# Splitting 32 TensorE products ahead of the branch: four tiles of the first batch from 512 to 256 columns, one pair of output tiles from 256 to 128

## The chip, the core and the metric

The kernel runs on one core of a Trainium2 chip. Its five engines run programs of their own and meet at semaphores: PE is TensorE (with PEld, its weight loads), DVE is VectorE, ACT is ScalarE, POOL is GpSimd, SP is SyncE, which here only issues transfers. The metric is the device time of one execution in microseconds (us), lower being better; the figure for a kernel is the median of its runs.

## The reference

The inputs are q, k and v (4 batches, 8 heads, 768 positions, 64 columns), a sorting network `sort_net` (4, 8, 8, 8), and the weights of a gated block. All is float32; the kernel multiplies in bfloat16.

```python
P = sort_net                                   # five Sinkhorn rounds
for _ in range(5):
    P = np.exp(P - P.max(-1)); P = P / P.sum(-1); P = P / P.sum(-2)
k_sorted = einsum('bhij,bhjcd->bhicd', P, k_b) # mixes the 8 blocks of 96 positions
v_sorted = einsum('bhij,bhjcd->bhicd', P, v_b)
attn = softmax(q_b @ k_sorted.T / 8) @ v_sorted   # inside each block of 96
x = attn as (4, 768, 512)
h = relu(x @ w_in)                             # 512 -> 1024 columns: u | v
v_n = layer norm of v over its 512 columns
gated = u * (w_spatial @ v_n + b_spatial)      # mixes the 768 positions
out = gated @ w_out                            # (4, 768, 512)
```

## The kernel before

The whole program is written out, with no loop on the chip. A string `ORDER` lists units, one word each (`VP:15:D:0:4`), and a Python function `u_XX` emits the instructions of each; the order in the string is the order in which every engine's own instructions stand. Four batches overlap: while one is in its attention, the one before it is in the gated block.

The units that matter here:

- **VP and VH** (`u_VP`, matmuls at L566) compute the v half of `x @ w_in` for one tile of 128 positions, 512 columns, as four products over the contraction that add up in one bank of PSUM. With `parts=2`, which is what VH asks for, the 512 columns are done as two runs of 256, each with its own four products and weight loads. Then one relu takes the 512 columns to SBUF, on ACT (L128) or on DVE (L130). Four of the six tiles of batch 0 are VP; the other 20 tiles of the kernel are VH.
- **OP** (`u_OP`, matmuls at L650) computes two tiles of 128 positions of `gated @ w_out`. Its last argument is the number of runs into which the 512 columns are cut: 2 everywhere.
- **SC** (L453) are scores, **AT** (L499) the products with the sorted v, **UP** (L612) the u half, **SP** and **SH** (L624, L680) the spatial product, **WT** (L535) a transpose of weights, **OH** (L700) the last output tiles of batch 3.

```python
for x in range(2):                     # u_OP
    for c in range(0, DM, w):          # w = 512 / parts
        for mc in range(FC):           # FC = 4
            nc.tensor.matmul(t[:, x, c:c + w], lhsT=gt[mc] of tile n0 + x, rhs=w_out_sb[:, mc, c:c + w],
                             start=(mc == 0), stop=(mc == FC - 1))
```

Every product has a weight load of its own in front of it, so a product that is cut in two becomes four instructions in place of two.

**The branch.** The kernel skips the maximum in the softmax, and the five-round network is checked afterwards: `CF` and `LF` (L746 to L751) turn the extreme values into a flag that every engine reads into a register. At `IF` in the string each engine compares and branches (L814). The usual path is the list behind `IF` (units OH, OI, OJ; on TensorE 36 products at L700 with their 36 weight loads). The other path computes everything again with the safe formulas, and it stands in between: on TensorE it is 1,832 products. The branch to the usual path is therefore a jump over that text. `BH`, at the head of the program (L843 in the profile), gives PE, DVE and ACT a hint that the branch is likely taken.

Of the kernel before, what the change touches and what calls it, by code (L numbers as in the profile page):

```python
# [22 lines left out]
SC:0:0:0:0 L:v:1:0:8 PD:1:0:4 VB:15:D:0:3 SC:3:0:1:0 AT:1:0:2:0 SC:0:0:2:1 AT:2:0:3:0 SC:3:0:0:1 PD:1:4:8 AT:1:0:0:0  # L23
KT:0:A:1:0 XT:14:D:0:0:2 AT:3:0:0:1 SC:1:0:3:1 KT:0:A:1:3 AT:2:0:2:1 VM:1:A:1:0 AT:3:0:3:1 VM:0:A:1:1 VM:2:D:1:3
L:q:1:0:8 VM:1:A:1:2 XT:16:A:0:1:2 L:wv AT:0:0:1:0 XT:17:A:0:1:0 KT:2:D:1:1 KT:1:A:1:2 QT:16:D:1:1 QT:10:D:1:3
QT:11:A:1:2 QT:17:D:1:0 XT:14:D:0:0:0 SC:1:1:1:0 L:wsa SC:0:1:2:1 SC:3:1:2:0 VP:15:D:0:4 ST:0:4 VP:14:D:0:3 L:wu
SC:1:1:0:0 SC:0:1:1:1 VP:15:D:0:1 L:wsb ST:0:3 WT:16:A:1 WT:17:D:0 VP:14:A:0:0 ST:0:1 VH:15:A:0:2 ST:0:0 WT:16:A:2
VC:1:0:4 L:q:2:0:8 VH:17:A:0:5 VC:1:4:8 PD:2:0:4 ST:0:2 ST:0:5 AT:1:1:0:0 LN:0:0:6 AT:0:1:1:0 UP:2:A:0:0:0
UP:3:A:0:1:0 BI LA:0:3 LA:0:4 AT:1:1:2:0 SC:2:1:0:1 UP:0:A:0:1:1 LA:0:1 AT:3:1:2:1 L:v:2:0:8 WT:14:A:3 L:k:2:0:8
LA:0:5 LA:0:2 WW:1:D:4 LA:0:0 SC:0:1:3:1 SC:3:1:3:0 UP:2:A:0:0:1 PD:2:4:8 AT:0:1:3:1 QP:A:2:0 SP:1:0:3 QP:A:2:3  # L30
# [12 lines left out]
OP:1:1:4:2 LA:2:5 SC:3:3:2:0 LA:2:0 LA:2:3 LA:2:1 SC:0:3:3:0 OP:2:1:2:2 AT:3:3:3:0 SP:0:2:1 GT:D:2:1 OE:A:1:4 XD:3:1  # L43
AT:1:3:2:0 SP:3:2:0 SP:0:2:2 CK XD:3:0 GT:P:2:0 OE:A:1:2 SP:2:2:3 VH:1:D:3:5:3 GT:D:2:3 VH:10:D:3:4 UP:3:A:3:1:1 CF:11
VH:12:A:3:2 VH:13:A:3:1 OS:1:2:0:2 LF VH:16:A:3:0 GT:D:2:2 OS:1:0:0:2:A UP:2:A:3:1:0 ST:3:1 ST:3:3 UP:0:A:3:0:0 ST:3:4
ST:3:5 OP:1:2:0:2 ST:3:2 ST:3:0 OP:3:2:4:2 LN:3:0:6 LA:3:3 OE:D:2:0 LA:3:4 OP:2:2:2:2 LA:3:0 LA:3:1 OE:A:2:2 LA:3:5
UP:0:A:3:0:1 OE:A:2:4 LA:3:2 OS:0:2:0:2 SH:12:3:2:0 SH:13:3:3:0 GH:P:3:3:0 SH:16:3:0:0 GH:D:3:2:0 SH:17:3:1:0
GH:P:3:0:0 SH:16:3:1:1 SH:12:3:2:1 OS:2:4 GH:P:3:1:0 SH:13:3:3:1 OS:2:0 GH:D:3:1:1 SH:17:3:0:1 OS:1:4 GH:D:3:3:1
OS:2:2 GH:P:3:0:1 GH:P:3:2:1 IF OH:16:3:2:0:512:0:4 OI:A:3:2:0:512 OH:12:3:3:0:512:0:4 OH:13:3:0:0:512:0:4
# [798 lines left out]
```

## Time and profile before

| what | value |
| --- | --- |
| median of 3 runs | 150.45 us (150.36 to 150.85) |
| the profiled execution, its own time | 150.09 us |
| its span, from the first to the last instruction of the program | 148.3 us |
| mean granted TensorE clock over the span | 0.997 |
| PE busy | 141.5 us, 95% of the span |
| DVE busy | 114.6 us, 77% |
| ACT busy | 85.9 us, 58% |
| POOL busy | 39.1 us, 26% |
| transfers of instructions, queue q8 | 14 of 16 KB each |

The span is 1.8 us shorter than the execution's own time; what lies around it are instructions that are not the kernel's. Busy times of PE are those of pipelined products, each of which is shown longer than the distance to the next one, so the distance between the starts of two products, from the chain of waits, is what a product costs when PE is the limit. The list of transfers has a queue per engine for instructions as well: q8 brings text of 16 KB a piece.

### The profile page before, as it was taken

The numbers are of one execution on the slowest core, as the hardware profiler recorded it, in microseconds if no ns is written. First come the engines' busy times: TensorE is split into PE (matmuls) and PEld (weight loads), VectorE is DVE, ScalarE is ACT, GpSimd is POOL, SyncE is SP. The second block draws the span as 40 slices with busy tenths as digits, with TensorE's granted clock in tenths as the row PEclk, the third lists the DMA queues.
The fourth block names the chain that finished last, engine by engine and source line by source line (L and its number), as shares of the span: only waits on it lengthen the run. The fifth ranks groups of instructions, "written<-read, shape, count | busy, mean of one in ns | idle before, by whom it ended". The sixth has DMA issues, their size and how long they took to land.

```text
span 148.3 us, 4108 instructions
## 1 busy us (share of the span) xinstructions
PE 141.5 (95%) x1691; PEld 100.8 (68%) x1691; DVE 114.6 (77%) x262; ACT 85.9 (58%) x126; POOL 39.1 (26%) x44
## 2 busy tenths in 40 slices
PE   6996999999999999999999999999999999999990
PEld 2445877867776657776877678768866876855760
DVE  3876899979987878867869879999568979846741
ACT  5348998987789547658793428756630055170130
POOL 6700699500000006991002640000003000004620
PEclk9999999999999999999999999999999999999998
DMA  3999999999999999799998999508203507007765
GB/s 93 263 205 203 205 209 201 208 221 242 231 248 216 204 216 241 111 197 223 207 201 162 214 243 254 125 0 85 26 0 76 176 6 277 0 2 301 273 235 197
DMA packets 36933, 25.93 MB, mean 175 GB/s; under 512 B 16624, under 2 KB 34032, under 8 KB 36912
## 3 DMA queue, kind: packets, MB, share of 16 engines
q0 software_dynamic: 14432, 12.19, 51.2%
q1 hardware_dynamic: 20832, 10.96, 31.1%
q10 hardware_dynamic: 1648, 2.49, 4.7%
q8 instruction: 14, 0.23, 0.6%
q14 instruction: 7, 0.06, 0.1%
HBM read 24.78 MB, written 6.29 MB: 210 GB/s over the span
## 4 chain that ended last, share of the span: by engine, by line
PE 83%; DVE 10%; ACT 2%; issue 1%; ACTq 0%; DVEq 0%
PE ps L624 16%; PE ps L566 15%; PE ps L612 14%; PE ps L650 11%; PE ps L680 5%; PE ps L499 4%; PE ps L394 4%; PE ps L453 4%; PE ps L700 3%; PE ps L421 3%; DVE x_sb L507 2%; DVE vb L124 1%; PE ps L529 1%; PE ps L535 1%; PE ps L325 1%
## 5 line engine op out<-in xcount | busy, mean ns | idle before, releaser
L641 POOL TENSOR_TENSOR gt<-z,u_sb 128x768 bf16<-128x768 f32 x7 | 11.4, 1645 | 68.5 <-DVE z L630 55.3
L458 ACT ACTIVATE ex_all<-ps 96x768 bf16<-96x768 f32 x32 | 23.7, 808 | 5.1 <-PE ps L453 4.0
L624 PE MATMUL ps<-wspT,v_sb 128*128 128x384 bf16 x144 | 25.1, 326 | 0.0
L566 PE MATMUL ps<-w_in_sb,xT 128*128 128x256 bf16 (+1 forms) x176 | 23.8, 283 | 0.0
L128 ACT ACTIVATE u_sb<-ps 128x768 bf16<-128x768 f32 x16 | 13.0, 811 | 17.3 <-PE ps L612 17.2
L612 PE MATMUL ps<-xT,w_in_sb 128*128 128x384 bf16 x128 | 23.0, 326 | 0.0
L507 DVE TENSOR_TENSOR x_sb<-ps,rec_all 96x512 bf16<-96x512 f32 x32 | 22.0, 686 | 1.1
L624 PEld LDWEIGHTS <-v_sb 128*128 128x128 bf16 x144 | 13.5, 98 | 8.3
L566 PEld LDWEIGHTS <-xT 128*128 128x128 bf16 x176 | 16.3, 98 | 4.0
L650 PE MATMUL ps<-w_out_sb,gt 128*128 128x256 bf16 x144 | 16.9, 273 | 0.0
L612 PEld LDWEIGHTS <-w_in_sb 128*128 128x128 bf16 x128 | 12.0, 98 | 7.0
L586 DVE BATCH_NORM_STATS2 stats<-v_sb 128x6 f32<-128x512 bf16 x24 | 16.2, 675 | 0.6 <-ACT v_sb L128 0.5
L122 ACT COPY o_sb<-ps 128x1024 f32<-128x1024 f32 (+2 forms) x11 | 8.9, 831 | 13.0 <-DVE z L686 7.0
L630 DVE TENSOR_TENSOR z<-ps,b_bc 128x768 f32<-128x768 f32 x12 | 11.5, 954 | 5.9 <-PE ps L624 5.9
L650 PEld LDWEIGHTS <-gt 128*128 128x128 bf16 x144 | 13.8, 98 | 2.0
L499 PEld LDWEIGHTS <-ex_all 96*128 96x128 bf16 x256 | 11.1, 97 | 2.6
L499 PE MATMUL ps<-vb,ex_all 96*128 96x65 bf16 x256 | 12.4, 193 | 0.1
L122 ACT CAST vm<-ps 128x768 bf16<-128x768 f32 x9 | 6.9, 807 | 9.5 <-PE ps L421 6.9
L693 POOL TENSOR_TENSOR gt<-z,u_sb 128x512 bf16<-128x512 f32 (+1 forms) x5 | 5.2, 1046 | 21.5 <-DVE z L686 21.5
L506 DVE RECIPROCAL rec_all<-ps 96x8 f32<-96x8 f32 x32 | 6.3, 195 | 5.6 <-PE ps L499 5.3
L130 DVE TENSOR_SCALAR v_sb<-ps 128x512 bf16<-128x512 f32 (+1 forms) x12 | 8.7, 727 | 1.6 <-PE ps L566 1.5
L236 PE MATMUL ps<-warm 128*128 128x512 bf16 (+2 forms) x34 | 8.6, 411 | 1.3 <-DVE warm L210 1.3
(100 smaller groups left out, 200.5 us busy)
## 6 DMA issues: line engine op xcount, KB each, us to landing
out_dram<-o_sb SPq DMA_DIRECT2D x7, 512.0 KB, 4.6
v_in<-in_v_dram POOLq DMA_DIRECT2D x4, 768.0 KB, 15.4
k_in<-in_k_dram POOLq DMA_DIRECT2D x4, 768.0 KB, 14.4
vb<-vm SPq DMA_DIRECT2D x24, 99.0 KB, 4.5
q_in<-in_q_dram POOLq DMA_DIRECT2D x3, 768.0 KB, 9.7
ws_in<-in_moe_w_spatial_dram POOLq DMA_DIRECT2D x2, 576.0 KB, 16.3
w_in_sb<-in_moe_w_in_dram POOLq DMA_DIRECT2D x2, 512.0 KB, 13.9
out_dram<-o_sb ACTq DMA_DIRECT2D x2, 512.0 KB, 4.1
```

What stands on the lines that cost most here:

```text
L122: nc.scalar.copy(out=out, in_=in_)
L128: nc.scalar.activation(out=out, in_=in_, func=AF.Relu)
L458: nc.scalar.activation(out=e_tile(b, hp, ih).rearrange("p h (x g) -> p h x g", g=G), in_=t[0:BLK, :, 0:HW].rearrange("p h (g x) -> p h x g ...
L499: nc.tensor.matmul(t[:, hh, ii * VW:ii * VW + D + 1], lhsT=e[:, c:c + 128], rhs=vb[b % 2][:, ih * NI + ii, 2 * hp + hh, 0:D + 1], start=Tr ...
L507: nc.vector.tensor_mul(out=x_sb[:, hp].rearrange("p i (h d) -> p h i d", h=2), in0=tv[:, :, :, 0:D], in1=_raw_ap(rec, 0, [rec.ap[0], [NI, ...
L566: nc.tensor.matmul(t[:, x, c:c + DH // parts], lhsT=st["xT", b][:, n // 3, kc, (n % 3) * 128:(n % 3 + 1) * 128], rhs=w_in_sb[:, kc, DH + c ...
L586: nc.vector.bn_stats(out=stats, in_=st["v_sb", b, n])
L612: nc.tensor.matmul(t[:, x, 0:HW], lhsT=w_in_sb[:, kc, mc * 128:(mc + 1) * 128], rhs=st["xT", b][:, ih, kc, :], start=(kc == 0), stop=(kc = ...
L624: nc.tensor.matmul(t[:, x, 0:HW], lhsT=st["v_sb", b, n][:, mc * 128:(mc + 1) * 128], rhs=wspT[:, 3 * x:3 * x + 3, n, :], start=(n == 0), s ...
L630: nc.vector.tensor_add(out=z.rearrange("p (x c) -> p x c", x=2), in0=t[:, :, 0:HW], in1=b_bc.rearrange("p (x c) -> p x c", x=2),)
L641: eng.tensor_mul(out=gt, in0=st["z", b, mc], in1=u)
L650: nc.tensor.matmul(t[:, x, c:c + w], lhsT=st["gt", b, mc][:, (n0 + x) * 128:(n0 + x + 1) * 128], rhs=w_out_sb[:, mc, c:c + w], start=(mc = ...
```

## The change

Five words of the string are changed; no function is.

```diff
-QT:11:A:1:2 QT:17:D:1:0 XT:14:D:0:0:0 SC:1:1:1:0 L:wsa SC:0:1:2:1 SC:3:1:2:0 VP:15:D:0:4 ST:0:4 VP:14:D:0:3 L:wu
-SC:1:1:0:0 SC:0:1:1:1 VP:15:D:0:1 L:wsb ST:0:3 WT:16:A:1 WT:17:D:0 VP:14:A:0:0 ST:0:1 VH:15:A:0:2 ST:0:0 WT:16:A:2
+QT:11:A:1:2 QT:17:D:1:0 XT:14:D:0:0:0 SC:1:1:1:0 L:wsa SC:0:1:2:1 SC:3:1:2:0 VH:15:D:0:4 ST:0:4 VH:14:D:0:3 L:wu
+SC:1:1:0:0 SC:0:1:1:1 VH:15:D:0:1 L:wsb ST:0:3 WT:16:A:1 WT:17:D:0 VH:14:A:0:0 ST:0:1 VH:15:A:0:2 ST:0:0 WT:16:A:2
...
-ST:3:5 OP:1:2:0:2 ST:3:2 ST:3:0 OP:3:2:4:2 LN:3:0:6 LA:3:3 OE:D:2:0 LA:3:4 OP:2:2:2:2 LA:3:0 LA:3:1 OE:A:2:2 LA:3:5
+ST:3:5 OP:1:2:0:2 ST:3:2 ST:3:0 OP:3:2:4:2 LN:3:0:6 LA:3:3 OE:D:2:0 LA:3:4 OP:2:2:2:4 LA:3:0 LA:3:1 OE:A:2:2 LA:3:5
```

The four tiles 4, 3, 1 and 0 of batch 0 take 8 products of 256 columns in place of 4 of 512. The tiles 2 and 3 of batch 2's output take 32 products of 128 columns in place of 16 of 256. The columns that stream through the array stay the same in number; 32 weight loads and 32 products are added, all of them ahead of `IF`. The rows of DVE, ACT, POOL and SP are the same before and after; those of PE go from 7052 to 7116.

PE in the first batch, at tile 4, behind the scores (xT holds the turned attention output, w_in_sb the weights, ps the bank that it adds up in):

```order
 L453 MATMUL ps_73<-qT_679,kt_all_100 128x6x16
 L566 LDWEIGHTS xT_536
-L566 MATMUL ps_73<-w_in_sb_92,xT_536 128x512
+L566 MATMUL ps_73<-w_in_sb_92,xT_536 128x256
...
+L566 LDWEIGHTS xT_536
+L566 MATMUL ps_73<-w_in_sb_92,xT_536 128x256
 L453 LDWEIGHTS kt_all_100
```

The products of a tile are halved in width, and as many again, each with its load, stand behind them before the next scores.

PE in the output of batch 2, tiles 2 and 3 (gt are the four gated chunks, w_out_sb the weights), before:

```order
L650 LDWEIGHTS gt_2085
L650 MATMUL ps_73<-w_out_sb_94,gt_2085 128x256
L650 LDWEIGHTS gt_2029
L650 MATMUL ps_73<-w_out_sb_94,gt_2029 128x256
L650 LDWEIGHTS gt_2191
L650 MATMUL ps_73<-w_out_sb_94,gt_2191 128x256
```

and now:

```order
L650 LDWEIGHTS gt_2101
L650 MATMUL ps_73<-w_out_sb_94,gt_2101 128x128
L650 LDWEIGHTS gt_2045
L650 MATMUL ps_73<-w_out_sb_94,gt_2045 128x128
L650 LDWEIGHTS gt_2207
L650 MATMUL ps_73<-w_out_sb_94,gt_2207 128x128
```

The four chunks are walked through four times for each tile in place of twice, at half the width.

PE at the branch and at the head of the usual path (v_sb is the normed v, wspT the turned spatial weights, spread and u_sb belong to the other path), before; now they are the same but for buffer numbers:

```order
L680 LDWEIGHTS v_sb_2119
L680 MATMUL ps_73<-wspT_93,v_sb_2119 128x256
L814 COMPARE_AND_BRANCH
L266 LDWEIGHTS spread_77
...
L814 UNCONDITIONAL_BRANCH
L700 LDWEIGHTS gt_2341
L700 MATMUL ps_73<-w_out_sb_94,gt_2341 128x512
```

The compare stands in row 3313 of PE before and in row 3377 now; the first row of the usual path moves from 6979 to 7043. Both move down by 64 rows and keep their distance.

## Prediction

> **What bounds the kernel now.** I read the page first: shares of busy time, granted clock, the chain of waits.
>
> ```profile
> span 148.3 us, 4108 instructions
> PE 141.5 (95%) x1691; PEld 100.8 (68%) x1691; DVE 114.6 (77%) x262; ACT 85.9 (58%) x126; POOL 39.1 (26%) x44
> PEclk9999999999999999999999999999999999999998
> PE 83%; DVE 10%; ACT 2%; issue 1%; ACTq 0%; DVEq 0%
> ```
>
> The chain that ended last runs over TensorE for 83% of the span, and the clock is full throughout. A share of the span is still a mean, so next comes the same account by stage: ahead of the first edit, around it, between the edits, the second edit, up to the branch, and behind it.
>
> ```profile
> core 0: us, PE busy (x) PEld busy (x) DVE busy (x) ACT busy (x) POOL busy (x), PEclk, DMA share, GB/s
> 0.00:31.30 31.30, 28.18 (x507) 19.80 (x508) 25.01 (x73) 23.91 (x37) 16.92 (x26) 1.00 1.18 199
> 31.30:37.00 5.70, 5.70 (x58) 3.46 (x56) 4.61 (x10) 4.79 (x7) 0.00 (x0) 1.00 1.18 237
> 37.00:125.10 88.10, 88.10 (x995) 64.38 (x993) 72.04 (x153) 51.08 (x73) 17.00 (x13) 1.00 0.87 166
> 125.10:130.30 5.20, 5.20 (x49) 4.63 (x48) 4.48 (x12) 1.32 (x3) 0.00 (x0) 1.00 0.00 0
> 130.30:139.40 9.10, 9.10 (x58) 5.48 (x56) 5.08 (x10) 2.73 (x3) 3.75 (x3) 1.00 0.59 224
> 139.40:148.30 8.90, 5.25 (x37) 3.08 (x34) 3.41 (x9) 2.03 (x4) 1.41 (x2) 0.95 0.52 190
> ```
>
> From 31.3 us to the branch and past it, TensorE has no idle moment. Both edits lie in stretches where it alone sets the pace: each nanosecond they add to its stream is a nanosecond of the end, and nothing they take off another engine would be seen. There is no idle time that a better order could win back either, ahead of 144 us.
>
> **The direct cost of the halved products.** What a product costs is the distance to the next one. The tail has all three widths, in three runs one behind the other.
>
> ```profile
> L700 PE MATMUL ps<-w_out_sb,gt 128*128 128x512 bf16 x16 | 3.6, 379 | 0.0
> L700 PE MATMUL ps<-w_out_sb,gt 128*128 128x256 bf16 x12 | 1.5, 272 | 0.0
> L700 PE MATMUL ps<-w_out_sb,gt 128*128 128x128 bf16 x8 | 0.6, 219 | 0.0
> 139.27:142.73 3.46, 3.46 (x19) 1.57 (x17) 1.94 (x5) 1.17 (x2) 1.41 (x2) 1.00 0.36 130
> 142.73:144.04 1.31, 1.31 (x14) 1.18 (x13) 0.69 (x3) 0.59 (x1) 0.00 (x0) 1.00 0.77 299
> 144.04:144.48 0.44, 0.44 (x10) 0.43 (x7) 0.44 (x2) 0.00 (x0) 0.00 (x0) 1.00 0.88 335
> ```
>
> The windows are cut at the start of the first product of each width. 16 products of 512 columns take 3.46 us, 216.2 ns each; 12 of 256 take 1.31 us, 109.2 ns; 8 of 128 take 0.44 us, 55 ns. So the first edit costs 16 x (2 x 109.2 - 216.2) = 0.035 us, and the second 32 x 55 - 16 x 109.2 = 0.01 us, or 0.03 us if each added product has the same 2 ns of its own as in the first. The sum is 0.05 us. Is there a gain or a larger loss in the places themselves?
>
> ```profile
> 31.34 1.83 PE ps L566 x8
> 33.62 0.97 PE ps L566 x4
> 34.59 0.67 PE ps L535 x12
> 35.26 1.74 PE ps L566 x12
> 60.13 0.87 PE ps L566 x8
> 61.62 0.98 PE ps L566 x8
> 125.10 5.24 PE ps L650 x48
> ```
>
> At 35.26 us four products of 512 and eight of 256 take 1.74 us, which is 4 x 216 + 8 x 109. The 0.97 us for four at 33.62 hold 0.1 us more, since scores stand ahead of them; the halved form pays the same behind scores (0.98 against 0.87 at 61.62 and 60.13). No side is won, so the lower bound is 0. For the second edit the nearest other row of 128 columns is the transpose at 34.59: 0.67 / 12 = 56 ns, which makes 0.04 us of it. The bounds of both edits together are 0 and 0.1 us, and I take 0.05, by the row of the same line and shape.
>
> A page sees it otherwise. The Trainium skill, "TensorE: Matmul & The Clock Gate", section "Back-to-back issue gap", says that in a stream of load and product pairs a product of 128 columns comes about every 81 ns, since the loads take part in the pace. The second edit would cost 32 x 81 ns less 1.75 us, an estimate of 0.84 us from that page, and the run would end at 151.3 us. The tail's 55 ns, for the same operands, speak against it.
>
> **The other engines.** DVE, ACT, POOL and SP keep their rows, with every transfer. A relu at L130 or L128 and the copy of the output tile get their tile some 10 to 30 ns later; DVE is busy 4.61 of 5.70 us in that stage and 4.48 of 5.20 in the second, and TensorE does not wait for it in either.
>
> **What moves: the branch.** 64 rows more stand ahead of the compare. This matters only through how TensorE's text is brought in. Queue q8 does that, and its window rows show when: the first row below is the page's, the second the stretch 41.9 to 135.3 us, then 135.3 to 135.4, 139.7 to 139.8 and 139.7 to 140.8.
>
> ```profile
> q8 instruction: 14, 0.23, 0.6%
> q8 instruction: 8, 0.13, 0.5%
> q8 instruction: 1, 0.02, 72.5%
> q8 instruction: 1, 0.02, 64.8%
> q8 instruction: 1, 0.02, 5.9%
> 41.99:135.36 93.37, 93.37 (x1006) 67.79 (x1004) 73.76 (x154) 51.46 (x73) 17.24 (x14) 1.00 0.77 149
> 0.00:133.79 133.79, 130.66 (x1618) 94.03 (x1619) 107.48 (x247) 83.83 (x122) 33.92 (x39) 1.00 0.90 166
> 0.00:137.68 137.68, 134.56 (x1641) 96.23 (x1642) 110.15 (x251) 83.83 (x122) 36.30 (x41) 1.00 0.90 171
> L814 PEldq COMPARE_BRANCH  x1: 481/481/481, 137.7 to 137.7; - x1
> 139.17 0.21 PEld L700 LDWEIGHTS <-gt 128*128 128x128 bf16 x2
> ```
>
> From 41.99 to 135.36 us eight pieces come for 1006 + 1004 instructions, 251 each; I take 256, a piece of 16 KB. A piece takes 5.9% of 16 engines over 1.1 us, 1.04 us. At 137.68 the sequencer branches while 1641 + 1642 = 3283 of the 3310 products and loads ahead of it have begun, so it leads the array by 27 instructions. The branch takes 0.48 us, and the first load of the usual path is at 139.17, right behind the last spatial product: the jump costs nothing. No piece comes between 135.4 and 139.7, so the piece of 135.36 must be that of the jump's target, brought ahead, and the one of 139.7, 1.6 us behind the end of the branch at 138.16, the piece after it. With the same 1.6 us, the piece of 135.36 was asked for at 133.8, when the sequencer stood at about 1618 + 1619 + 27 = 3264, some 46 instructions ahead of the branch: there a piece of text begins. The spread of that figure is about 20, from the delay.
>
> Now the change. The pieces stay where they are and the branch moves down by 64: it stands 110 instructions behind the start of its piece (46 before), still inside it, so the target should be brought as before, with more time to spare. The target lies 3669 instructions on (3666 rows and three waits that are not shown), 14 pieces and 85: 131 into its piece before, 195 now. Some 61 instructions are left in it, and the usual path has 74. Its last 13 thus come from the next piece, which before served only what follows the program. That piece is asked for at the jump and landed at 140.8. The sequencer needs it when 61 - 27 = 34 instructions, 17 products, have begun: 139.27 + 3.46 + 0.11 = 142.8 us. The cover is 2.0 us, and 20 instructions fewer still leave 0.9. I cost it at nothing. Ahead of the branch the pieces come every 8 to 18 us and take 2.6 with their delay, so 64 rows do not thin that cover.
>
> **Sum.** 148.3 + 0.05 for the span, with 1.8 us around it as before: 150.14 for an execution like the profiled one at 150.09. The median of the runs lies 0.36 above that one, so I forecast 150.5 us.
>
> **The rivals.**
>
> 1. *The next piece is asked for only when the sequencer runs into its end.* The request falls at 142.8, and 1.6 + 1.04 us later, at 145.4, the text is there; the array has run dry at 30 products begun, 139.27 + 3.46 + 1.31 + 2 x 0.055 = 144.15. Price 1.25 us, 151.7 us; with the piece's end 20 instructions earlier 0.1, and nothing if the path just fits. Against it: at 139.7 a piece came without any need. Chance 0.12.
> 2. *The target is not brought ahead any more*, since the branch stands elsewhere in its piece. Then at 138.16 the sequencer waits 1.6 + 1.04 us and 0.3 to start again: first load at 141.1, not 139.17, 1.9 us, 152.4 us. It decides if the hint works only close behind a piece's start, or if the piece ends in the 64 rows. For it: one branch is all I have. Against it: the figure of 46. Chance 0.09. The Trainium skill, "Runtime: NRT & Kernel Launch", section "Instruction fetch mechanics", says that text is fetched in 16 KiB blocks of 256 instructions and that a taken branch whose target is outside the window waits for a fetch. The trace agrees on the size, 251 by count, and not on the wait, 0.48 us and all of it hidden.
> 3. *Loads set the pace at 128 columns*, 151.3 us. Chance 0.03.
> 4. *Faster, behind the end.* Before, some 47 instructions of the target's piece are left behind the program's last row (256 - 131 - 78), so what follows it may run into the next piece and ask for one more; now this happens inside the usual path, hidden. If the end waited for such a request, at most the 1.8 us around the span could shrink; half of it makes 149.6 us. For it: only that the text behind the end moves. Against it: no row shows a wait there. Chance 0.17.
>
> **Numbers.** My forecast has a chance of 0.55; 0.04 stay for a loss I have not named. About 0.3%, 0.45 us, is what a measurement of this kernel can tell from no change. The forecast lies within that but for a few hundredths on each side. Faster: rival 4 and 0.02 of the forecast, 0.19. Slower: rivals 1, 2, 3, the unnamed and 0.02, less the short forms of rival 1, 0.27. Same: the rest, 0.54. The likeliest case by itself spans 150.2 to 150.9. The range reaches down to the middle of rival 4, 149.6, and up to rival 1's full price, 151.7, which leaves out rival 2 and part of 4, less than 2 in 10.
>
> **What would show it.** Right: distances of 109 ns between the new products of L566 and of 55 to 56 ns between those of L650, no idle TensorE between the last L680 and the first L700 product, a q8 piece some 64 instructions earlier than the last one before the branch, 15 pieces in place of 14 with the last near 144 us. Wrong: a gap at the branch of about 2 us (rival 2), a gap among the last dozen products of L700 (rival 1), 80 ns a product at L650 (rival 3), or an equal span with a shorter execution (rival 4).

## The result, and the profile after

The changed kernel takes 151.70 us (median of 6 runs, 151.17 to 152.21), the one before 150.41 us (6 runs beside it): a ratio of 1.0088, 95% interval 1.0068 to 1.0108. It is slower by 1.3 us, and the loss that the prediction priced was 0.05 us. Ratios, and the times of the runs below, leave out executions more than 1.5% above the fastest of the same kernel, which are three of six in one kernel (warm64) and one of ten in another (rows48). The profiled execution of the changed kernel took 152.21 us, the slowest of its six, against 150.09.

The page of the changed kernel, its span, busy times, clock, chain of waits and text queue:

```profile
span 150.4 us, 4171 instructions
PE 142.4 (95%) x1722; PEld 102.7 (68%) x1723; DVE 114.6 (76%) x262; ACT 86.0 (57%) x126; POOL 39.0 (26%) x44
PEclk9999999999999999999999999999999999999997
PE 81%; DVE 10%; DMA 2%; ACT 2%; issue 1%; ACTq 0%; DVEq 0%
q8 instruction: 15, 0.25, 0.7%
```

Busy times and clock are the old ones. Two things are new: a share of the chain that waits for a transfer (of sorted v, below), and a fifteenth piece of text. The chain of waits in order of time (start, length, what), at the edits and where it differs:

```profile
31.61 1.85 PE ps L566 x16
33.91 0.98 PE ps L566 x8
35.56 1.75 PE ps L566 x16
89.78 3.70 DMA vb<-vm
126.14 5.28 PE ps L650 x64
140.52 5.22 PE ps L700 x36
```

The three pieces of the first batch were 1.83, 0.97 and 1.74 us long and grew by 0.04 together; the outputs were 5.24 and grew by 0.04. Both edits cost 0.08 us. The usual path starts 1.08 us later than in the profiled execution before (140.25 against 139.17, below). 0.27 us of that was there before the first edit, 0.08 are the edits, and 0.73 came where TensorE waited near 93 us for a copy of the sorted v (`vb<-vm`). Of the twelve kernels below two show such a wait in their profiled execution, one of 0.3 us and one of 2.8, which has troubles of its own; I take it and the 0.27 for this execution's luck, though no run tests that, and the median for the measure.

The branch, the head of the usual path and the new products:

```profile
L814 PEldq COMPARE_BRANCH  x1: 395/395/395, 138.8 to 138.8; - x1
140.25 0.21 PEld L700 LDWEIGHTS <-gt 128*128 128x128 bf16 x2
L650 PE MATMUL ps<-w_out_sb,gt 128*128 128x128 bf16 x32 | 1.9, 219 | 0.0
```

The branch is as short as before (0.48 then), the last spatial product starts at 140.25 us as well, and the 36 products behind the branch show no idle time. TensorE loses nothing there. The rest of the loss lies behind it. These are the transfers of output, with their size and the median time from issue to landing; first before:

```profile
out_dram<-o_sb SPq DMA_DIRECT2D x3, 256.0 KB, 2.1
out_dram<-o_sb ACTq DMA_DIRECT2D x3, 128.0 KB, 1.9
out_dram<-o_sb SPq DMA_DIRECT2D x1, 128.0 KB, 1.9
```

and now:

```profile
out_dram<-o_sb SPq DMA_DIRECT2D x3, 256.0 KB, 3.3
out_dram<-o_sb ACTq DMA_DIRECT2D x3, 128.0 KB, 3.2
out_dram<-o_sb SPq DMA_DIRECT2D x1, 128.0 KB, 3.0
```

The same transfers land 1.1 to 1.3 us later. In the changed kernel the text queue, in the windows 144.7 to 144.8 and 144.7 to 145.8, has

```profile
q8 instruction: 1, 0.02, 60.5%
q8 instruction: 1, 0.02, 5.5%
```

the fifteenth piece: it starts in the first tenth and takes 5.5% of 16 engines over 1.1 us, 0.97 us. The row shows it as one packet, which I take to be the work of one engine; no view names the engine of a packet. How the output then ends shows in the windows (the last two columns are the busy share of the 16 transfer engines and GB/s), before:

```profile
145.50:146.60 1.10, 0.00 (x0) 0.00 (x0) 0.00 (x0) 0.00 (x0) 0.00 (x0) 1.00 0.95 331
147.00:147.80 0.80, 0.00 (x0) 0.00 (x0) 0.00 (x0) 0.00 (x0) 0.00 (x0) 0.74 0.00 0
```

and now:

```profile
147.00:147.80 0.80, 0.00 (x0) 0.00 (x0) 0.00 (x0) 0.00 (x0) 0.00 (x0) 1.00 0.94 324
147.80:148.70 0.90, 0.00 (x0) 0.00 (x0) 0.00 (x0) 0.00 (x0) 0.00 (x0) 1.00 0.07 24
```

Before, all engines work to the end and stop together. Now they stop at about 147.8 us, and for 0.9 us more the share is 0.07, about one engine in sixteen: one engine works off its part of the output alone, and the program waits for it. That it is the one that had the piece of text is inferred from the sizes, 0.97 us for the piece and 0.9 us for the rest; the last experiment below puts a packet of data in the piece's place.

### The profile page after: what moved, and what is told of

Read it like the earlier page. It is cut to its first block, busy times and chain, and to the rows that moved or that the text cites. A ratio compares the mean times of both kernels' runs of the same rounds, so it can differ in the third digit from the quotient of the medians.

```text
span 150.4 us, 4171 instructions
## 1 busy us (share of the span) xinstructions
PE 142.4 (95%) x1722; PEld 102.7 (68%) x1723; DVE 114.6 (76%) x262; ACT 86.0 (57%) x126; POOL 39.0 (26%) x44
## 4 chain that ended last, share of the span: by engine, by line
PE 81%; DVE 10%; DMA 2%; ACT 2%; issue 1%; ACTq 0%; DVEq 0%
PE ps L624 16%; PE ps L612 14%; PE ps L566 13%; PE ps L650 11%; PE ps L680 5%; PE ps L499 4%; PE ps L394 4%; PE ps L700 3%; PE ps L453 3%; PE ps L421 3%; DMA vb<-vm 2%; DVE x_sb L507 2%; DVE vb L124 1%; PE ps L529 1%; PE ps L535 1%
## 5 line engine op out<-in xcount | busy, mean ns | idle before, releaser
L566 PE MATMUL ps<-w_in_sb,xT 128*128 128x256 bf16 x192 | 23.8, 273 | 0.0
L566 PEld LDWEIGHTS <-xT 128*128 128x128 bf16 x192 | 17.8, 98 | 2.9
L650 PE MATMUL ps<-w_out_sb,gt 128*128 128x256 bf16 (+1 forms) x160 | 16.9, 262 | 0.0
L236 PE MATMUL ps<-warm 128*128 128x512 bf16 (+2 forms) x33 | 9.2, 436 | 1.3 <-DVE warm L210 1.3
```

The lines of the kernel that those rows point to most:

```text
L566: nc.tensor.matmul(t[:, x, c:c + DH // parts], lhsT=st["xT", b][:, n // 3, kc, (n % 3) * 128:(n % 3 + 1) * 128], rhs=w_in_sb[:, kc, DH + c ...
L650: nc.tensor.matmul(t[:, x, c:c + w], lhsT=st["gt", b, mc][:, (n0 + x) * 128:(n0 + x + 1) * 128], rhs=w_out_sb[:, mc, c:c + w], start=(mc = ...
```

## The experiments

**Theory F**: the 64 rows push the end of the usual path out of its piece of text; the sequencer then asks for one more piece while the last output flows; that packet of about 1 us delays one engine's share of the output. Its rivals are P, the added products cost the time; C, each further row or a third piece costs wherever it falls; T, the fetch of text does something other than occupy an engine. Twelve kernels were run; all are edits of the order string unless shown otherwise. The quoted texts are what was expected before each run.

| kernel | rows ahead of the branch, against before | pieces of text | last outputs on ACT's queue, issue to landing, us | ratio to before, 95% interval |
| --- | --- | --- | --- | --- |
| the change | +64 | 15 | 3.2 | 1.0088 (1.0068 to 1.0108) |
| vh_only | +32 | 14 | 1.9 | 1.0010 (0.9984 to 1.0036) |
| op_only | +32 | 14 | 1.9 | 1.0013 (0.9997 to 1.0029) |
| rows48 | +48 | 14 | 1.9 | 1.0019 (0.9991 to 1.0047) |
| other64 | +64 | 15 | 3.2 | 1.0107 (1.0082 to 1.0133) |
| warm64 | +64 | 15 | 3.4 | 1.0266 (1.0216 to 1.0315) |
| rows96 | +96 | 15 | 3.2 | 1.0088 (1.0071 to 1.0104) |
| rows128 | +128 | 14 | 1.9 | 1.0016 (0.9998 to 1.0034) |
| taken64 | 0, both edits kept | 14 | 1.9 | 1.0009 (0.9992 to 1.0025) |
| long_late | 0 | 14 | 2.2 | 1.0024 (1.0003 to 1.0045) |
| wide_late | 0 | 14 | 2.4 | 1.0013 (0.9995 to 1.0032) |
| long_early | 0 | 14 | 1.9 | 0.9997 (0.9974 to 1.0020) |
| one_16k | 0 | 14 | 3.2 | 1.0096 (1.0068 to 1.0125) |

**Each edit alone.**

```diff
-VP:15:D:0:4 ... VP:14:D:0:3 ... VP:15:D:0:1 ... VP:14:A:0:0
+VH:15:D:0:4 ... VH:14:D:0:3 ... VH:15:D:0:1 ... VH:14:A:0:0
```

> The first edit alone: four tiles of batch 0 as VH, the output pair as before. 32 rows more ahead of the branch, not 64. Theory F (the added text pushes the end of the usual path into a further piece, so TensorE asks for one more 16 KB piece while the last output is on its way, and that piece of about 1 us stands in front of output packets): about 83 instructions of the target's piece are left and path and end need 78, so no third piece near the end, 150.4 us, 14 pieces. Rival P (the halved products themselves cost the 1.3 us, each of the 32 added ones its share): half of it, 151.0 us.

```diff
-OP:2:2:2:2
+OP:2:2:2:4
```

> The second edit alone: the output pair as four runs of 128. Also 32 rows more ahead of the branch. Theory F: as for the first edit alone, 150.4 us, 14 pieces. Rival P: if the 128-column products are the costly ones, up to 151.7 us; if all added ones are, 151.0 us.

They took 150.47 and 150.48 us, and neither costs more than its interval can hide; if the two added up they would make 0.2%, and 0.65% with the upper ends of both intervals, not 0.9%. P is out as far as either edit alone goes.

**Text moved without the change's products.** First by cutting the warm-up products at the head.

```diff
-DM:10:3:384 ... DM:10:4:512 ... DM:10:13:512 ... DM:10:4:256 ... DM:12:4:512 ... DM:13:6:512
+DM:10:6:192 ... DM:10:8:256 ... DM:10:26:256 ... DM:10:6:170 ... DM:12:8:256 ... DM:13:12:256
```

> Both edits undone, and 64 rows added elsewhere: the warm-up products at the head are cut into 32 more of smaller width, with the same columns in all. They feed nothing. The branch stands where it stands in the changed kernel. Theory F: 151.7 us, 15 pieces, the last starting near 144.7 us of the span, the last output landing some 0.8 to 1.1 us later after its issue than in the kernel before. Rival P: 150.4 us, since the products of the change are not there.

154.54 us: much more than either theory said. The chain of waits of its profiled execution, which took 156.25 us, shows why it can't be used:

```profile
60.74 6.19 DMA vb<-vm
66.97 0.31 PE ps L499 x5
```

TensorE waits there for a copy of the sorted v and is idle for 2.8 us, and its granted clock is 0.93 from 67 to 90 us. The end does look as F says, 15 pieces and 3.4 us to the landing, but the time is no test. Why the copy comes late with the warm-up cut is open. So the text was moved by other products, close to the branch:

```diff
-OP:1:2:0:2 ... OP:3:2:4:2
+OP:1:2:0:4 ... OP:3:2:4:4
```

> Neither edit of the change, but 64 rows from other products: the output pairs of batch 1 (tiles 2 and 3 of the last pair list) and batch 2's tiles 4 and 5 as four runs of 128. The branch and the usual path stand where they stand in the changed kernel. Theory F: 151.6 us, 15 pieces, the last one starting between 143 and 145.5 us, TensorE without a gap, the last output landing 1 us or more later after its issue than before. Rival P (it is the two edits, together): 150.5 us.

The two pairs are tiles 0 and 1 and tiles 4 and 5 of batch 2; the expectation misnames the first. Neither edit of the change is in it, the rows ahead of the branch are as many, and the loss is there: 151.87 us. Its text queue and its last outputs:

```profile
q8 instruction: 15, 0.25, 0.6%
out_dram<-o_sb ACTq DMA_DIRECT2D x3, 128.0 KB, 3.2
out_dram<-o_sb SPq DMA_DIRECT2D x1, 128.0 KB, 3.0
```

**The change's products without the move.**

```diff
-OP:1:0:0:2 ... OP:3:0:2:2 ... OP:1:0:4:2 ... OP:0:1:0:2   (of the changed kernel)
+OP:1:0:0:1 ... OP:3:0:2:1 ... OP:1:0:4:1 ... OP:0:1:0:1
```

> Both edits kept, and 64 rows taken out elsewhere: four output pairs of the earlier batches as one run of 512 columns. The branch stands in the row where it stands in the kernel before. Theory F: 150.4 us, 14 pieces, none after the one behind the branch. Rival P: 151.6 us.

150.41 us, beside 150.33 of before. Both edits are in it and cost nothing that can be told from zero. It is also a form of the change without the loss.

**Where the piece ends.**

```diff
-VP:15:D:0:4 ... VP:14:D:0:3 ... OP:2:2:2:2   (of the kernel before)
+VH:15:D:0:4 ... VH:14:D:0:3 ... OP:2:2:2:4
```

> The second edit and half of the first (tiles 4 and 3): 48 rows more ahead of the branch. About 67 instructions of the target's piece are left, and the usual path needs 74. Theory F: it still runs into the next piece, only some 16 instructions later; a third piece starts near 145 us, while the last outputs flow, and costs 0.6 to 1.3 us: 151.0 to 151.7 us. If the piece's end lies further than I count, it costs nothing, 150.5 us.

The second half of that came true: 14 pieces within the span, 150.46 us. (A fifteenth starts at 149.6 us, behind the span's end at 148.6, and delays nothing.) The step lies between 48 and 64 rows. By the prediction's own count, 131 instructions into the piece before, 77 are left with 48 rows, so the 74 of the path fit, and 61 are left with 64 rows, so they don't. The step lies where that count puts it; the 67 of this expectation was too low.

```diff
-OP:3:2:4:2   (of the changed kernel)
+OP:3:2:4:4
```

> The change with a further output pair (batch 3 of the string's banks, tiles 4 and 5 of batch 2) as four runs of 128: 96 rows more ahead of the branch than before. Theory F: the path runs into its second piece some 32 instructions earlier, so the third piece starts near 142 us and is done near 143, before the last outputs are issued; it costs little: 150.5 to 150.9 us, with 15 pieces. Rival C (a third piece costs its time wherever it comes, for instance by stopping TensorE's sequencer): 151.7 us. Rival P: more halved products, 152.3 us.

This expectation failed: the piece came at 143.4 us, not near 142, and the loss stayed, 151.59 us. In time and landing it is C's result, and a part of C's example is there too, as the list of waits shows:

```profile
PEld L700 <- issue: 0.5, 1, 0.5
```

The loads of the usual path stop for 0.52 us ahead of 142.24, when 11 of the 36 have begun, and the path's products take 5.58 us from the first start to the last end, 5.37 before. The view names no cause; by the count only 29 instructions of the target's piece are left here, so this is where TensorE would need the next piece, and I take it to wait for text. That is 0.2 us of the loss. The fifteenth piece also took longer than in the changed kernel, 1.44 us against 0.97. The next run tests the other form of C, that each added row costs.

```diff
-OP:1:2:0:2 ... OP:3:2:4:2   (of the changed kernel)
+OP:1:2:0:4 ... OP:3:2:4:4
```

> The change with two further output pairs as four runs of 128: 128 rows more than before ahead of the branch, 64 added products. The head of the usual path then falls at the very start of a piece of text, and all of it fits. Theory F: no third piece near the end, 150.5 us, although more products are cut than in any kernel so far; the last output lands as soon after its issue as before. Rival C (each added row costs, or any move of the branch by more than about 50 rows): 152 us or more.

With 128 rows, the most products of all, the loss is gone: 150.75 us, a ratio of 1.0016 whose interval takes in 1. The path now starts near the head of a piece and fits. Its chain of waits at the outputs, its text queue and its last outputs:

```profile
125.71 5.36 PE ps L650 x96
q8 instruction: 14, 0.23, 0.7%
out_dram<-o_sb ACTq DMA_DIRECT2D x3, 128.0 KB, 1.9
out_dram<-o_sb SPq DMA_DIRECT2D x1, 128.0 KB, 1.9
```

96 products in place of 48 take 5.36 us in place of 5.24, and that is all. Row count as such costs nothing; a third piece near the end does. Why the piece of rows96 delayed the landings as much as the later one is open: from 144.8 to 145.5 us, behind it, the share of the engines is only 0.45, which would have left a late engine time to catch up. So the other half of C, that a third piece costs wherever it falls, is not refuted for places among the last outputs.

**A stand-in for the piece.** If the packet is what counts and not that it is text, any long packet should do. The next four leave TensorE's program as it was before. First two rows of one partition on SP, behind the third output transfer of the path, of lengths that don't divide; they go to spare memory that nothing reads.

```diff
+nc.sync.dma_start(out=spare[0:1, 0:4607], in_=wspT flat [0:1, 0:4607])
+nc.sync.dma_start(out=spare[1:2, 0:4093], in_=w_in_sb flat [0:1, 0:4093])
-OJ:3:0:0:512:S
+OJ:3:0:0:512:S ZL
```

> The kernel before, with its text of TensorE untouched, and two transfers more on SP behind the third output transfer of the usual path: 9.2 and 8.2 KB of one partition each, lengths that do not divide, so that each should be a single long packet on a single transfer engine. They take the part of the third piece of text, while the last outputs flow. Theory F (a long packet on one engine holds up that engine's share of the output): 151.0 to 151.5 us, the last outputs landing 0.5 to 1.2 us later. Rival T (it is the fetch of text as such, by what it does to TensorE's sequencer or to the end of the program): 150.4 us.

```diff
+nc.sync.dma_start(out=wide[0:128, 0:68], in_=w_in_sb[0:128, 0, 0:68])
-OJ:3:0:0:512:S
+OJ:3:0:0:512:S ZW
```

> As the kernel with the two long packets, but the same 17 KB as 128 short rows over all engines, at the same place. Theory F: every engine is held up by about a sixteenth, 150.4 to 150.6 us. If it is the bytes or the further issues on SP that cost, the same as with the long packets.

```diff
-IF OH:16:3:2:0:512:0:4
+IF ZL OH:16:3:2:0:512:0:4
```

> The same two long packets, ahead of the first output transfer of the usual path on SP, so that they are done before the last outputs flow. Theory F: 150.4 to 150.6 us. If a long packet costs wherever it stands: 151 us or more.

These three are weak. Early packets cost nothing (150.27 us), late ones 0.5 us (150.75), which is less than I expected, and the same bytes in short rows 0.3 (150.57). The intervals of the last two overlap, and so do the landings, 2.2 and 2.4 us. The two packets took 0.35 and 0.31 us, not 1 us together, so they were a smaller load than the piece. The last run made one packet of the piece's own size, from HBM:

```diff
+nc.sync.dma_start(out=spare, in_=k as one row of 4093 float32)
-OJ:3:0:0:512:S
+OJ:3:0:0:512:S ZD
```

> The kernel before with one transfer more on SP behind the third output transfer of the usual path: 16,372 bytes from one place of k to a spare place in HBM, of a length that does not divide, so that it should be one packet on one engine, as the piece of text is. The two packets from SBUF took 0.66 us together and started at 144.8 us, the piece of text took 0.97 from 144.7. Theory F: if the single packet takes about 1 us of one engine from about 144.8 us, the last outputs land 0.8 to 1.3 us later and one engine is left working alone at the end (DMA share 0.06); 151.1 to 151.7 us. Rival T (the fetch does something else besides): no more than the 128 short rows cost, 150.6 us.

151.89 us, 1.0096. Its transfers and the windows at its end:

```profile
out_dram<-o_sb ACTq DMA_DIRECT2D x3, 128.0 KB, 3.2
out_dram<-o_sb SPq DMA_DIRECT2D x1, 128.0 KB, 3.4
spare<-in_k_dram SPq DMA_DIRECT2D x1, 16.0 KB
146.60:147.40 0.80, 0.00 (x0) 0.00 (x0) 0.00 (x0) 0.00 (x0) 0.00 (x0) 1.00 0.82 287
147.40:148.30 0.90, 0.00 (x0) 0.00 (x0) 0.00 (x0) 0.00 (x0) 0.00 (x0) 1.00 0.07 24
```

The picture of the changed kernel without a change of TensorE's program: outputs 1.3 to 1.5 us late, a share of one engine for the last 0.9 us at 24 GB/s. The packet starts at 145.0 us and takes 1.32 us, so it is done 2 us ahead of the last landing: the end waits for the output behind it, not for the packet itself. One packet of 16 KB, while the last output flows, is enough for the whole loss, and T is not needed. (The issue took SP 0.75 us, so one output of 256 KB was issued about half a microsecond later than it would have been. That is not the loss: in long_late the same output is issued at 144.4 us too, and the landings on ACT's queue are 2.2 us.)

## Why the prediction was wrong, point by point

- *What bounds the kernel.* Right as far as TensorE goes. But the claim that no idle time could be won back reached only to 144 us, and behind that the transfers of output bound the end. The stage from the last product to the end of the span, 3.8 us of the profiled execution before, was never costed.
- *The direct cost*, 0.05 us with bounds 0 and 0.1: right, measured 0.08. The 81 ns for a product of 128 columns, which the Trainium skill gives in "TensorE: Matmul & The Clock Gate", section "Back-to-back issue gap", did not show: 32 of them in place of 16 products of 256 added 0.04 us.
- *The other engines*: right, their busy times are the old ones.
- *The branch*: right. The target was brought ahead at 46 and at 110 instructions into the piece, and in rows128 at 174; rival 2 is out. In the Trainium skill, "Runtime: NRT & Kernel Launch", section "Instruction fetch mechanics", a crossing into the next block is mostly hidden. For TensorE it was in the changed kernel; in rows96 its loads stopped for 0.52 us.
- *The piece's end*: the count was right (61 instructions left for 74, a piece more, at 144.7 us). One margin was misread: with 20 instructions fewer the text is needed after 7 products, at 139.27 + 7 x 0.216 = 140.8 us, so the cover is nothing, not 0.9 us. In rows96, with 32 fewer, TensorE's loads did stop. **The step that failed** is "I cost it at nothing", said of the piece that the end of the path needs. It asked only whether TensorE would wait for the text, found 2.0 us of cover, and did not ask what the *next* request, the one that entering a piece sets off, would stand in front of. The prediction itself named that request, "15 pieces in place of 14 with the last near 144 us", and listed it as a sign of being right. The output transfers at 144 to 146 us, which the end waits for, were its victims: they landed 1.1 to 1.3 us later.
- *Rival 1* names the time that came, 151.7, and not its cause: there is no gap in the last products, and the text they needed had been there. Its mechanism is refuted, so that 151.70 is also the top of the forecast's range is luck.
- *Rival 3* is out by the 0.04 us. *Rival 4*: the time around the span is 1.8 us in the profiled execution before (150.09 - 148.3) and in the changed one (152.21 - 150.4), so nothing was won there; rows48, where the request falls behind the program's end, and rows128, where there is none, have the ratios 1.0019 and 1.0016.
- The chance that I gave to no change, 0.54, and the 0.04 for a loss not named, rested on one trace of transfers in which the last seven microseconds had never held a piece of TensorE's text. A transfer was priced by who waits for it, not by whom it delays.

## What to carry to other kernels

Text is a transfer too. Where a program ends in output, count the instructions from its last jump to its end, and keep the end out of a new piece of text, by adding or taking rows ahead: the same products cost 0.9% or nothing by where they leave the end. When a request of any kind moves into the last microseconds, ask on which engine it lands and what that engine still has to deliver; a load that is 1 us on one of sixteen engines delayed the whole end here by 1 us and more, though the mean share hardly moved.

## What was not expected of the hardware

- One packet of 16 KB took 0.97 us as text in the changed kernel, 0.88 in other64 and 1.32 as data, and the time grew by 1.3 to 1.6 us (1.0088, 1.0107 and 1.0096). 17 KB as 128 short rows cost at most 0.3%.
- The delay didn't wear off. In rows96 the piece started between 143.4 and 143.5 us and took 1.44 us, so it was done 0.9 us ahead of the last issue of output at 145.7, and the landings were still 3.2 us. Why is open.
- With the warm-up products cut into 32 more the kernel took 4 us longer. One execution shows a wait of 2.8 us for a copy, from 64 to 67 us; whether that is the cause was not followed up.
